# Attention and a gated feed-forward on one core: batch 3 by casting loads, batch 4's loads held until tile 2 runs, the tails of batches 0 and 1 moved ahead of batch 2's rounds

## The chip, the core and the metric

The kernel runs on one core of one Trainium2 chip. A core has five engines, each with an instruction stream of its own: TensorE (PE in the profile) multiplies matrices, VectorE (DVE), ScalarE (ACT) and GpSimd (POOL) work on elements, and SyncE (SP) here does nothing but issue DMA transfers. An engine runs its stream in order; if an instruction waits, everything behind it on the same engine waits too. Sixteen DMA engines move data between device memory and the core's on-chip memory (SBUF); the accumulators of TensorE lie in PSUM. The metric is device time in microseconds (us), lower is better. A time given for the kernel is the median of several executions.

## The reference

Eight batches, eight heads, 576 positions, head width 64. The inputs and the output are float32. Attention is causal by blocks of 64 positions, and its result is the input of a gated feed-forward:

```python
scores = (1 / sqrt(64)) * q @ k.transpose(0, 1, 3, 2)       # (8, 8, 576, 576)
scores = where(block_i >= block_j, scores, -1e9)            # blocks of 64 positions
attn   = exp(scores - max); attn = attn / (sum(attn) + 1e-9)
x      = (attn @ v), heads side by side                     # (8 * 576, 512)
gate   = maximum(x @ w_gate, 0)                             # w_gate: 512 x 1536
val    = x @ w_val                                          # w_val:  512 x 1536
out    = (gate * val) @ w_out                               # w_out: 1536 x 512
```

## The kernel before

**Units of work.** The first 512 positions of a batch are its main part, the last 64 its tail. Attention on the main part goes by head pairs: a *round* r = 4 * batch + pair covers two heads of one batch, 32 rounds in all. A round has scores (`visit`, L364: four chunks of keys by two heads, into PSUM tiles called `sc`, `one` and `ffnp`), exponentials on ScalarE (L387 for 512 columns of both heads, L393 for the rest), zeroing of the masked corners (L686, VectorE), products with v (`head_av`, L500, or `both_av`, L514; matmuls L491), a division by the row sums on VectorE (L456, L457) into a tile `xnat`, and a transpose of `xnat` into a quarter of `xT`, the feed-forward's input: on TensorE (`to_xT_pe`, L529) for batches 0 and 1, by a DMA transpose that SP issues (`to_xT_dma`, L540, recorded as L543) from batch 2 on. The tail of a batch is one visit for all heads (`tail_visit` L399, `tail_av` L464, matmuls L412 and L471), whose result goes by a DMA transpose (L485) into `xTt`.

**The feed-forward** runs in nine tiles (`ffn_gen`, L562): tile j below 8 is the main part of batch j, tile 8 all tails together. A tile has 96 matmuls of 512 columns for gate and val (L568; f runs over 12 slices of the 1536, c over the four quarters of `xT`) and 48 for the output (L625). ScalarE makes the relu (L578), VectorE the product gate * val, called `hT` (L583), and the copies of the output (L645, L656, L659), which ScalarE's queue stores (L554). In tiles 0 and 1 the first two slices are opened over quarters 0 and 1, then 2, then 3 of `xT`; from tile 2 on every slice needs all four quarters at once, so the fourth matmul of tile 2 needs the quarter of batch 2's last round.

**Order.** All engines run in the written order (`manual_schedule`, L691). The generator is a clock: one step is one feed-forward matmul, 144 steps a tile. `run(base, events)` (L780) sorts a list of (place, function) pairs and calls each function when the clock reaches base + place. A round is spread over such places by `round_at(p, r, av, to_xT, after)` (L785): scores and first exponentials at p, the others shortly after, products with v at `av`, the transpose at `to_xT`. `tail_at(p, b, av)` (L806) does it for a tail. Rounds 4 to 7 (batch 1) lie in the second half of tile 0, rounds 8 to 11 (batch 2) in tile 1, rounds 12 to 15 (batch 3) in tile 2, and so on: attention of batch j + 1 is laid between the matmuls of tile j.

**Loads.** There are two ways to bring a batch in.

- *Staged* (class `Early`, L107): SP issues plain float32 loads into a ring of ten `stage` tiles (L105), and POOL, ScalarE or VectorE cast them to bf16. `load_qk` (L127) takes q and k for n heads, `load_v` (L136) and `load_v_chunks` (L144) v, `load_tails` (L154) the last 64 rows. Batches 0 and 1 are then transposed on TensorE (`pe_mains` L232, `pe_tails` L251); batches 2 and 3 by DMA transposes on SP into tiles called `perm` (`transpose`, L205, recorded as L209; `transpose_tails`, L215) and, since q and k were loaded four positions to a row, put in order by copies on VectorE and POOL (`unpermute`, L221, recorded as L223).
- *Casting* (`load_qkv`, L264): POOL issues DMA transfers that read float32 and write bf16 (L276), five for each of q, k and v. SP then issues four DMA transposes (`dma_transposes`, L283): the main parts of q and k (L286), and their tails (L290). Batches 4 to 7 come this way; the loads of batch b + 1 are recorded in tile b - 1 at places 4 (q and k) and 46 (v), the transposes at 66. POOL has by then nothing else to do, so it runs ahead of the clock until something makes it wait.

SBUF buffers: `q_bf`/`k_bf` (L99) and their tails `q_bt`/`k_bt` (L102) have two buffers each, and `qTm`, `kTm`, `qTt`, `kTt` and `v_bf` two by batch parity, so that batch 3 takes what batch 1 used. `psum_ffn` has three banks, shared by gate, val, output, products with v and one part of each round's scores.

**Weights.** Gate and val weights come first, in halves; then batch 1's first four heads of q and k, `w_out` in three parts of two loads (`load_w_out`, L318; cast by `cast_w`, L321, the last quarter of the last part by VectorE at place 112.05), batch 1's v and its second four heads. In the kernel before, SP's order there is: two parts of `w_out`, v of heads 0 to 3, the third part, q and k of heads 4 to 7, v of heads 4 to 7, batch 0's tails, batch 2's q and k.

Of the kernel before, what the change touches and what calls it, by code (L numbers as in the profile page):

```python
# [12 lines left out]
AX = mybir.AluOpType  # L13
# [4 lines left out]
def kernel(  # L18
# [10 lines left out]
    nc = tc.nc  # L29
# [234 lines left out]
    def load_qkv(b, which):  # L264
        for t in which:
            src = (q, k, v)[t]
            for c in range(NCH):
                n = 128 if c < 4 else 64
                if t == 2:
                    dst = v_bf[b % 2][:n, c, :, 0:64]  # L270
                else:
                    if (b, 0) not in bfs:
                        bfs[b, 0], bfs[b, 1] = new_bf(), new_bt()
                    dst = bfs[b, 0][t][:, 512 * c : 512 * c + 512] if c < 4 else bfs[b, 1][t]
                    dst = dst.rearrange("p (h d) -> p h d", h=8)
                nc.gpsimd.dma_start(  # L276
                    dst,
                    src[b, :, 128 * c : 128 * c + n, :].rearrange("h p d -> p h d"),
                )

# [37 lines left out]
    def load_w_out(i):  # L318
        return load_w(wo[i], moe_w_out, 512 * i)
# [242 lines left out]
    def ffn_gen():  # L562
        for j in range(B + 1):
# [17 lines left out]
            def hidden(gate_sb, val):  # L581
                h = sb.tile([128, 512], BF, name="hT", bufs=13)
                nc.vector.tensor_tensor(out=h, in0=gate_sb, in1=val, op=AX.mult)  # L583
                hT.append(h)
# [106 lines left out]
    with tc.manual_schedule(engines={E.PE, E.DVE, E.Activation, E.Pool, E.SP}):  # L691
# [60 lines left out]
        w_out = [load_w_out(i) for i in range(2)]  # L752
        e1.load_v(0, 4)
        w_out.append(load_w_out(2))
        e1.load_qk(4, 4)
        e1.load_v(4, 4)
        e0.load_tails((0, 1))
        e0.load_tails((2,))
# [7 lines left out]
        e1.cast_v(0, 4, pool)  # L766
# [3 lines left out]
        e1.cast_qk(4, 4, (pool, None))  # L770
        e1.cast_v(4, 4, pool)
        e0.cast_tails((pool, pool))
        e0.cast_v_tail(pool)
# [57 lines left out]
        def tails_2():  # L831
            e1.cast_tails((pool, pool))
            e1.cast_v_tail(pool)
            e2.cast_tails((pool, pool))
            e2.transpose_tails()
            e2.cast_v_tail(pool)
# [4 lines left out]

        def load_3():
            e3 = early[3] = Early(3)
            e3.load_qk(0, 4)
            e3.load_tails((0, 1))
            e3.load_qk(4, 4)
            e3.load_tails((2,))
            e3.load_v_chunks(0)
            e3.load_v_chunks(1)

        def mains_3(h0):
            early[3].cast_qk(h0, 4, (pool, pool))
            if h0 == 4:
                early[3].cast_tails((pool, pool))

        def v_3():
            e3 = early[3]
            for g in range(2):
                e3.cast_v_chunks(g, pool)
            e3.cast_v_tail(pool)  # L860

        def un(b, hp, engs=(dve, dve)):
            return lambda: early[b].unpermute(hp, engs)

        def mains_2(h0):
            e2.load_v_chunks(h0 // 4)
            e2.cast_qk(h0, 4, (pool, pool))
            e2.transpose(h0 // 4)

        def load_tails():  # L870
            e1.load_tails((0, 1))
            e1.load_tails((2,))
            e2.load_tails((0, 1))
            e2.load_tails((2,))

        events = round_at(96, 4, (112, 112.1), (116, pe_xT), (6, 11))
        events += round_at(104, 5, (127, 127.1), (131, pe_xT), (6, 15))
        events += round_at(128.5, 6, (139, 140), (146, pe_xT), (4, 9))
# [6 lines left out]
            (120.2, lambda: e1.cast_qk(4, 4, (None, act))),  # L885
            (123, lambda: e1.pe_mains(2, (dve, act))),
            (125, lambda: e1.pe_mains(3, (dve, act))),
            (128, lambda: mains_2(0)),
            (142, lambda: e0.pe_tails((dve, act))),
            (143, lambda: mains_2(4)),  # L890
# [3 lines left out]
        events = tail_at(24, 0, (40, 44)) + tail_at(116, 1, (132, 136))  # L894
        for r, p in ((8, 41), (9, 58), (10, 75), (11, 92)):
            events += round_at(p, r, (p + 21, p + 25), (p + 25, to_xT_dma))
        events += [
            (88, lambda: e1.pe_tails((dve, act))),
            (20, lambda: store.pop()()),
            (25, un(2, 0, (dve, pool))),  # L900
            (28, un(2, 1, (dve, pool))),
            (46, v_2),
            (47, load_3),
            (52, un(2, 2, (dve, pool))),
            (56, un(2, 3, (dve, pool))),
            (60, tails_2),
            (66, lambda: mains_3(0)),
            (81, lambda: early[3].transpose(0)),
            (82, lambda: mains_3(4)),
            (101, lambda: early[3].transpose(1)),  # L910
            (118, lambda: early[3].transpose_tails()),
            (121, un(3, 0, (dve, pool))),
            (125, un(3, 1, (dve, pool))),
            (137, v_3),
        ]
        run(144, events)
        for b in range(3, B):
# [6 lines left out]
            if b == 3:  # L924
                events.append((2, un(3, 2, (dve, pool))))
                events.append((40, un(3, 3, (dve, pool))))
            if b + 1 < B:
                for at, which in ((4, (0, 1)), (46, (2,))):
                    events.append((at, lambda b=b, w=which: load_qkv(b + 1, w)))
                events.append((66, lambda b=b: dma_transposes(b + 1)))  # L930
# [31 lines left out]
```

The softmax here doesn't subtract the row's maximum and nothing guards it: scores larger than these inputs give would overflow.

## Time and profile before

| | |
|---|---|
| median of 9 runs | 374.96 us (371.48 to 376.3) |
| the profiled execution | 373.58 us, span 371.6 us, mean granted TensorE clock 0.998 |
| PE busy | 356.0 us, 96% of the span, 2963 matmuls |
| DVE, ACT, POOL busy | 174.9 us (47%), 169.8 us (46%), 112.7 us (30%) |
| device memory | 37.75 MB read, 9.44 MB written, 127 GB/s over the span |

The page shows one execution in several views: busy time by engine; the span in 40 slices; the DMA queues; the chain of work that ended last; the costliest groups of instructions with the idle time of the engine in front of them and what ended it; the DMA issues with their time to landing. Asked further, the trace gives the waits (who waited for whom), a timeline of one engine in a window, busy time by window, and single DMA issues. "SPq" and "POOLq" are issuing queues. A matmul of 512 columns is shown at about 379 ns, but successive ones overlap: 96 of them in a row take 20.72 us in the chain, 0.2158 us each. That 0.2158 us is one step of the clock of the order above where nothing else lies between.

With that step, tile 0 starts at 17.78 us in the timeline of TensorE, tile 1 at 61.24, tile 2 at 104.57 and tile 3 at 148.83. From there each tile takes about 38.8 us (in the chain, the first matmul of tile 4 is at 189.56 and that of tile 5 at 228.33).

### The profile page before, as it was taken

What the parts mean: (1) busy time and instruction counts of PE and PEld (TensorE: products, weight loads), DVE (VectorE), ACT (ScalarE), POOL (GpSimd) and SP (SyncE); (2) the same over time, 40 slices, a digit from 0 to 9 for tenths busy, and PEclk for the clock granted to TensorE, in tenths of its full rate; (3) what the DMA queues carried; (4) which work ended last, traced back from release to release, by engine and by line L of the source; (5) the groups of instructions that cost most, each with busy time, mean ns of one, the idle gap of its engine ahead of it and who ended that gap; (6) DMA issues with size and microseconds to landing.
All of it is one profiled execution on the core that took longest, in us unless ns stands there. A gap on an engine that the chain in (4) does not pass through costs nothing.

```text
span 371.6 us, 7467 instructions
## 1 busy us (share of the span) xinstructions
PE 356.0 (96%) x2963; PEld 176.5 (47%) x2963; DVE 174.9 (47%) x399; ACT 169.8 (46%) x278; POOL 112.7 (30%) x142
## 2 busy tenths in 40 slices
PE   6799989999969999899999999999999999999996
PEld 2444445544534545344554455444544454444443
DVE  4744465775534554354345533554354543423432
ACT  5733746667235652456445544553465323302310
POOL 5776645285079920930066004000000000000000
PEclk9999999999999999999999999999999999999999
DMA  8999999999889999997499747956200120020014
GB/s 253 279 347 357 319 258 311 211 203 248 136 155 127 119 145 163 162 126 142 114 96 138 125 115 86 57 77 137 79 17 14 56 88 7 0 86 28 0 36 108
DMA packets 145187, 51.35 MB, mean 138 GB/s; under 512 B 124544, under 2 KB 139136, under 8 KB 145152
## 3 DMA queue, kind: packets, MB, share of 16 engines
q1 hardware_dynamic: 83616, 34.62, 43.6%
q0 software_dynamic: 56256, 7.08, 38.5%
q10 hardware_dynamic: 5280, 9.18, 7.7%
q8 instruction: 23, 0.38, 0.5%
q14 instruction: 12, 0.10, 0.1%
HBM read 37.75 MB, written 9.44 MB: 127 GB/s over the span
## 4 chain that ended last, share of the span: by engine, by line
PE 80%; DMA 15%; SPq 1%; ACT 1%; issue 0%; POOL 0%; DVE 0%; ACTq 0%; POOLq 0%
PE ffnp L568 45%; PE ffnp L625 22%; DMA stage<-in_moe_w_gate_dram 5%; PE ffnp L491 4%; DMA xT<-xnat 4%; DMA stage<-in_k_dram 3%; PE sc L378 3%; DMA stage<-in_moe_w_out_dram 3%; PE ffnp L471 2%; PE one L378 1%; SPq L139 1%; DMA stage<-in_v_dram 1%; PE sc L412 1%; PE one L412 0%; ACT gate_sb L578 0%
## 5 line engine op out<-in xcount | busy, mean ns | idle before, releaser
L583 DVE TENSOR_TENSOR hT<-gate_sb,ffnp 128x512 bf16<-128x512 bf16 x106 | 72.8, 687 | 95.7 <-PE ffnp L568 83.5
L578 ACT ACTIVATE gate_sb<-ffnp 128x512 bf16<-128x512 f32 x108 | 64.7, 601 | 105.4 <-PE ffnp L568 101.8
L568 PE MATMUL ffnp<-xT,wg 128*128 128x512 bf16 x384 | 103.7, 379 | 6.1 <-DMA xT<-xnat 4.7
L625 PE MATMUL ffnp<-wo,hT 128*128 128x512 bf16 (+1 forms) x444 | 102.0, 373 | 0.2 <-DVE ob L645 0.2
L568 PE MATMUL ffnp<-xT,wv 128*128 128x512 bf16 x376 | 100.5, 379 | 0.0
L568 PEld LDWEIGHTS <-wg 128*128 128x128 bf16 x432 | 40.2, 98 | 48.9 <-issue 5.3
L568 PEld LDWEIGHTS <-wv 128*128 128x128 bf16 x432 | 40.0, 98 | 49.2 <-issue 6.1
L625 PEld LDWEIGHTS <-hT 128*128 128x128 bf16 x444 | 40.5, 98 | 41.5 <-issue 0.8
L387 ACT ACTIVATE attnT<-sc 128x1024 bf16<-128x1024 f32 x56 | 57.0, 1039 | 0.2 <-issue 0.2
L659 DVE COPY ob<-ffnp 128x512 f32<-128x512 f32 (+1 forms) x35 | 23.7, 677 | 39.1 <-PE ffnp L625 39.1
L276 POOL DMA_DIRECT2D v_bf<-in_v_dram x20 | 17.2, 882 | 67.5 <-PE ffnp L471 67.5
L491 PEld LDWEIGHTS <-attnT 128*128 128x128 bf16 x640 | 26.2, 98 | 14.0 <-DVE xnat L457 3.5
L456 DVE RECIPROCAL recip<-ffnp 128x4 f32<-128x4 f32 (+1 forms) x73 | 13.1, 179 | 33.3 <-PE ffnp L491 21.5
L491 PE MATMUL ffnp<-v_bf,attnT 128*128 128x65 bf16 x570 | 26.4, 194 | 0.0
L393 ACT ACTIVATE attnT<-one 128x256 bf16<-128x256 f32 x28 | 10.7, 383 | 33.7 <-PE ffnp L378 28.8
L457 DVE TENSOR_TENSOR xnat<-ffnp,recip 128x256 bf16<-128x256 f32 x57 | 24.2, 424 | 2.5 <-DMA xT<-xnat 0.5
L433 ACT ACTIVATE attnTt<-one 64x256 bf16<-64x256 f32 x8 | 3.0, 377 | 33.5 <-PE ffnp L412 26.9
L378 PE MATMUL sc<-qTm,kTm 64*128 64x512 bf16 (+1 forms) x168 | 17.4, 305 | 0.0
L378 PEld LDWEIGHTS <-kTm 64*128 64x128 bf16 x224 | 9.6, 94 | 15.6 <-issue 11.7
L424 ACT ACTIVATE attnTt<-sc 128x1024 bf16<-128x1024 f32 x16 | 15.6, 1013 | 0.0
L223 POOL COPY kTm<-perm 128x512 bf16<-128x512 bf16 x8 | 9.2, 1175 | 19.0 <-DMA perm<-k_bf 13.6
L276 POOL DMA_DIRECT2D k_bf<-in_k_dram x16 | 14.3, 935 | 0.6 <-DMA v_bf<-in_v_dram 0.3
(87 smaller groups left out, 263.9 us busy)
## 6 DMA issues: line engine op xcount, KB each, us to landing
out_dram<-ob ACTq DMA_DIRECT2D x32, 256.0 KB, 2.7
stage<-in_moe_w_gate_dram SPq DMA_DIRECT2D x6, 512.0 KB, 8.9
stage<-in_moe_w_val_dram SPq DMA_DIRECT2D x6, 512.0 KB, 8.7
stage<-in_q_dram SPq DMA_DIRECT2D x6, 512.0 KB, 6.5
stage<-in_k_dram SPq DMA_DIRECT2D x6, 512.0 KB, 6.7
stage<-in_moe_w_out_dram SPq DMA_DIRECT2D x6, 512.0 KB, 8.6
stage<-in_v_dram SPq DMA_DIRECT2D x20, 128.0 KB, 5.7
stage<-in_v_dram SPq DMA_DIRECT2D x8, 256.0 KB, 6.5
```

The costliest lines, as they stand in the source:

```text
L276: nc.gpsimd.dma_start(dst, src[b, :, 128 * c : 128 * c + n, :].rearrange("h p d -> p h d"),)
L378: nc.tensor.matmul(where[c].rearrange("p (c n) -> p c n", n=128), kTm[b % 2][head_of(hh), c, hp, :], qTm[b % 2][head_of(hh), c:4, hp, :], ...
L387: return lambda: nc.scalar.activation(at[:, :, lo : lo + 512], sc, AF.Exp, scale=scale)
L424: return lambda: nc.scalar.activation(at[:, :, 2 * i : 2 * i + 2, 0:256], main[i].rearrange("p g (h n) -> p g h n", h=2), AF.Exp, scale=scale,
L456: nc.vector.reciprocal(recip, av[:, :, 64])
L457: nc.vector.tensor_tensor(out=out, in0=av[:, :, 0:64], in1=recip.to_broadcast([rows, n, 64]), op=AX.mult,)
L491: nc.tensor.matmul(av[:, p, :], at[:, col : col + 128], v_bf[b % 2][:, c, h, :], start=(p == 0), stop=(c == p), skip_group_check=True,)
L568: nc.tensor.matmul(to, (wg, wv)[t][f // 4][:, c, 128 * (f % 4) : 128 * (f % 4) + 128], x[:, c], start=(c == 0), stop=(c == 3),)
L578: nc.scalar.activation(gate_sb, gate, AF.Relu)
L583: nc.vector.tensor_tensor(out=h, in0=gate_sb, in1=val, op=AX.mult)
L625: nc.tensor.matmul(op, hT[f][:, 128 * s : 128 * (s + 1)], wo[f // 4][:, f % 4, n0:n1], start=(f == lo), stop=(f == hi - 1),)
L659: nc.vector.tensor_copy(ob, op)
```

## The change

The changed kernel loads batch 3 as batches 4 to 7 are loaded, by casting DMA on POOL and four DMA transposes on SP, recorded in tile 1 (q and k at place 59, v at 92, the transposes at 119). `load_3`, `mains_3`, `v_3` and batch 3's un-permuting copies go. The casting loads of batch 4's q and k are recorded at place 9 of tile 2 instead of 4, and the first of them waits for the VectorE product (`hT`) recorded last before it. The tails of batches 0 and 1 are both loaded, cast and transposed before tile 1, and their attention lies at places 24 and 40 of tile 1 (before: 24 and 116); batch 2's rounds begin at 54, 67, 80 and 94 (before: 41, 58, 75, 92). All of `w_out` is loaded and cast ahead of batch 1's v. Batch 1's second four heads of q and k are loaded and cast two at a time; the products with v of round 4 move from place 112 to 120, round 6 from 128.5 to 126, the transposes of head pair 3 from 125 to 129. The un-permuting copies of batch 2 move from places 25, 28, 52, 56 to 43, 46, 50, 56, its tails from 60 to 90.

```diff
--- before.py
+++ after.py
@@ -261,7 +261,9 @@
             for t in range(2):
                 evac[t]((qTt, kTt)[t][self.b % 2][:, 0:4, :], tp[:, t])
 
-    def load_qkv(b, which):
+    products = []
+
+    def load_qkv(b, which, behind=None):
         for t in which:
             src = (q, k, v)[t]
             for c in range(NCH):
@@ -273,10 +275,12 @@
                         bfs[b, 0], bfs[b, 1] = new_bf(), new_bt()
                     dst = bfs[b, 0][t][:, 512 * c : 512 * c + 512] if c < 4 else bfs[b, 1][t]
                     dst = dst.rearrange("p (h d) -> p h d", h=8)
-                nc.gpsimd.dma_start(
+                ins = nc.gpsimd.dma_start(
                     dst,
                     src[b, :, 128 * c : 128 * c + n, :].rearrange("h p d -> p h d"),
                 )
+                after(ins, behind)
+                behind = None
 
     bfs = {}
 
@@ -580,7 +584,9 @@
 
             def hidden(gate_sb, val):
                 h = sb.tile([128, 512], BF, name="hT", bufs=13)
-                nc.vector.tensor_tensor(out=h, in0=gate_sb, in1=val, op=AX.mult)
+                products.append(
+                    nc.vector.tensor_tensor(out=h, in0=gate_sb, in1=val, op=AX.mult)
+                )
                 hT.append(h)
 
             first = 0
@@ -749,13 +755,14 @@
         e1, e2 = Early(1), Early(2)
         e1.load_qk(0, 4)
         ffn(23)
-        w_out = [load_w_out(i) for i in range(2)]
+        w_out = [load_w_out(i) for i in range(3)]
         e1.load_v(0, 4)
-        w_out.append(load_w_out(2))
-        e1.load_qk(4, 4)
+        for h0 in (4, 6):
+            e1.load_qk(h0, 2)
         e1.load_v(4, 4)
-        e0.load_tails((0, 1))
-        e0.load_tails((2,))
+        for e in (e0, e1):
+            e.load_tails((0, 1))
+            e.load_tails((2,))
         e2.load_qk(0, 4)
         e2.load_qk(4, 4)
         for g in range(2):
@@ -763,14 +770,16 @@
         e1.cast_qk(0, 4, (pool, None))
         cast_w(w_out[0], pool)
         cast_w(w_out[1], pool)
-        e1.cast_v(0, 4, pool)
         cast_w(w_out[2][:1], pool)
         last_w = [[a[:, c : c + 1] for a in w_out[2][1]] for c in range(2)]
         cast_w(last_w[:1], pool)
-        e1.cast_qk(4, 4, (pool, None))
+        e1.cast_v(0, 4, pool)
+        for h0 in (4, 6):
+            e1.cast_qk(h0, 2, (pool, None))
         e1.cast_v(4, 4, pool)
-        e0.cast_tails((pool, pool))
-        e0.cast_v_tail(pool)
+        for e in (e0, e1):
+            e.cast_tails((pool, pool))
+            e.cast_v_tail(pool)
         place = [32]
 
         def upto(p):
@@ -829,8 +838,6 @@
         early = {2: e2}
 
         def tails_2():
-            e1.cast_tails((pool, pool))
-            e1.cast_v_tail(pool)
             e2.cast_tails((pool, pool))
             e2.transpose_tails()
             e2.cast_v_tail(pool)
@@ -838,26 +845,6 @@
         def v_2():
             e2.cast_v_chunks(0, pool)
             e2.cast_v_chunks(1, pool)
-
-        def load_3():
-            e3 = early[3] = Early(3)
-            e3.load_qk(0, 4)
-            e3.load_tails((0, 1))
-            e3.load_qk(4, 4)
-            e3.load_tails((2,))
-            e3.load_v_chunks(0)
-            e3.load_v_chunks(1)
-
-        def mains_3(h0):
-            early[3].cast_qk(h0, 4, (pool, pool))
-            if h0 == 4:
-                early[3].cast_tails((pool, pool))
-
-        def v_3():
-            e3 = early[3]
-            for g in range(2):
-                e3.cast_v_chunks(g, pool)
-            e3.cast_v_tail(pool)
 
         def un(b, hp, engs=(dve, dve)):
             return lambda: early[b].unpermute(hp, engs)
@@ -868,50 +855,43 @@
             e2.transpose(h0 // 4)
 
         def load_tails():
-            e1.load_tails((0, 1))
-            e1.load_tails((2,))
             e2.load_tails((0, 1))
             e2.load_tails((2,))
 
-        events = round_at(96, 4, (112, 112.1), (116, pe_xT), (6, 11))
+        events = round_at(96, 4, (120, 120.1), (125, pe_xT), (6, 11))
         events += round_at(104, 5, (127, 127.1), (131, pe_xT), (6, 15))
-        events += round_at(128.5, 6, (139, 140), (146, pe_xT), (4, 9))
+        events += round_at(126, 6, (138.2, 139), (146, pe_xT), (4, 9))
         events += round_at(138, 7, (148, None), (153, pe_xT), (3, 8))
         events += [
             (80, lambda: e1.cast_qk(0, 4, (None, dve))),
             (93, lambda: e1.pe_mains(0, (dve, act))),
             (95, lambda: e1.pe_mains(1, (dve, act))),
             (112.05, lambda: cast_w(last_w[1:], dve)),
-            (120.2, lambda: e1.cast_qk(4, 4, (None, act))),
+            (119, lambda: e1.cast_qk(4, 2, (None, act))),
+            (120.2, lambda: e1.cast_qk(6, 2, (None, act))),
             (123, lambda: e1.pe_mains(2, (dve, act))),
-            (125, lambda: e1.pe_mains(3, (dve, act))),
+            (129, lambda: e1.pe_mains(3, (dve, act))),
             (128, lambda: mains_2(0)),
             (142, lambda: e0.pe_tails((dve, act))),
+            (142, lambda: e1.pe_tails((dve, act))),
             (143, lambda: mains_2(4)),
             (143, load_tails),
         ]
         run(0, events)
-        events = tail_at(24, 0, (40, 44)) + tail_at(116, 1, (132, 136))
-        for r, p in ((8, 41), (9, 58), (10, 75), (11, 92)):
-            events += round_at(p, r, (p + 21, p + 25), (p + 25, to_xT_dma))
+        events = tail_at(24, 0, (37, 39)) + tail_at(40, 1, (55, 58))
+        for r, p in ((8, 54), (9, 67), (10, 80), (11, 94)):
+            events += round_at(p, r, (p + 21, p + 24), (p + 24, to_xT_dma))
         events += [
-            (88, lambda: e1.pe_tails((dve, act))),
             (20, lambda: store.pop()()),
-            (25, un(2, 0, (dve, pool))),
-            (28, un(2, 1, (dve, pool))),
-            (46, v_2),
-            (47, load_3),
-            (52, un(2, 2, (dve, pool))),
+            (43, un(2, 0, (dve, pool))),
+            (46, un(2, 1, (dve, pool))),
+            (46.5, v_2),
+            (50, un(2, 2, (dve, pool))),
             (56, un(2, 3, (dve, pool))),
-            (60, tails_2),
-            (66, lambda: mains_3(0)),
-            (81, lambda: early[3].transpose(0)),
-            (82, lambda: mains_3(4)),
-            (101, lambda: early[3].transpose(1)),
-            (118, lambda: early[3].transpose_tails()),
-            (121, un(3, 0, (dve, pool))),
-            (125, un(3, 1, (dve, pool))),
-            (137, v_3),
+            (59, lambda: load_qkv(3, (0, 1))),
+            (90, tails_2),
+            (92, lambda: load_qkv(3, (2,))),
+            (119, lambda: dma_transposes(3)),
         ]
         run(144, events)
         for b in range(3, B):
@@ -921,12 +901,16 @@
             for i, p in enumerate((27, 50, 73, 96) if b == 3 else (2, 32, 62, 92)):
                 r = 4 * b + i
                 events += round_at(p, r, (p + 20, p + 24), (p + 24, to_xT_dma))
-            if b == 3:
-                events.append((2, un(3, 2, (dve, pool))))
-                events.append((40, un(3, 3, (dve, pool))))
             if b + 1 < B:
-                for at, which in ((4, (0, 1)), (46, (2,))):
-                    events.append((at, lambda b=b, w=which: load_qkv(b + 1, w)))
+                for at, which in ((9, (0, 1)), (46, (2,))):
+                    events.append(
+                        (
+                            at,
+                            lambda b=b, w=which: load_qkv(
+                                b + 1, w, products[-1] if b == 3 and w == (0, 1) else None
+                            ),
+                        )
+                    )
                 events.append((66, lambda b=b: dma_transposes(b + 1)))
             run(144 * (b - 1), events)
         ffn(10**6)
```

## The prediction

> **What bounds the kernel now.** I read the page's busy shares first, then TensorE's waits, its timeline where they lie, and SP's timeline over the longest.
>
> ```profile
> PE 356.0 (96%) x2963; PEld 176.5 (47%) x2963; DVE 174.9 (47%) x399; ACT 169.8 (46%) x278; POOL 112.7 (30%) x142
> ```
>
> TensorE is the bound. The change keeps every matmul, so it can only give or take idle time in front of them; TensorE's waits name what there is.
>
> ```profile
> PE ffnp L568 <- DMA xT<-xnat: 4.7, 4, 3.2
> ...
> PE ffnp L568 <- POOL wg L323: 1.0, 1, 1.0
> PE ffnp L238 <- ACT k_bf L168: 0.8, 1, 0.8
> ```
>
> TensorE's timeline (start, us, instruction, idle before):
>
> ```profile
> 47.57 1.25 PE L625 MATMUL ffnp<-wo,hT 128*128 128x512 bf16 x4 [0.17 <-DVE ob L645]
> 49.00 0.40 PE L537 MATMUL ffnp<-ident,xnat 128*128 128x128 bf16 x4 [0.18 <-DVE xnat L457]
> ...
> 51.96 0.40 PE L238 MATMUL ffnp<-ident,k_bf 128*128 128x128 bf16 x4 [0.83 <-ACT k_bf L168]
> ...
> 109.25 0.38 PE L568 MATMUL ffnp<-xT,wg 128*128 128x512 bf16 x1 [3.18 <-DMA xT<-xnat]
> ...
> 149.63 0.38 PE L568 MATMUL ffnp<-xT,wg 128*128 128x512 bf16 x1 [0.42 <-DMA xT<-xnat]
> ...
> 151.55 0.38 PE L568 MATMUL ffnp<-xT,wg 128*128 128x512 bf16 x1 [0.89 <-DMA xT<-xnat]
> 152.17 0.38 PE L568 MATMUL ffnp<-xT,wg 128*128 128x512 bf16 x1 [0.24 <-DMA xT<-xnat]
> ```
>
> The big one is the fourth matmul of tile 2, which waits for round 11's quarter of xT. Its xnat was ready at 98.37 (VectorE's timeline: L457 at 97.95 for 0.42). SP's timeline shows why it came late:
>
> ```profile
> 83.35 6.50 SPq L149 DMA_DIRECT2D stage<-in_v_dram  x4
> 89.95 1.76 SPq L217 DMA_TRANSPOSE qTt<-q_bt  x1
> 91.81 2.02 SPq L217 DMA_TRANSPOSE kTt<-k_bt  x1
> 93.93 1.22 SPq L543 DMA_TRANSPOSE xT<-xnat  x1
> 95.24 1.26 SPq L209 DMA_TRANSPOSE perm<-q_bf  x1
> 96.59 1.29 SPq L209 DMA_TRANSPOSE perm<-k_bf  x1
> 97.97 3.57 SPq L543 DMA_TRANSPOSE xT<-xnat  x2
> 101.63 1.26 SPq L209 DMA_TRANSPOSE perm<-q_bf  x1
> 102.99 1.53 SPq L209 DMA_TRANSPOSE perm<-k_bf  x1
> 104.61 2.24 SPq L543 DMA_TRANSPOSE xT<-xnat  x1
> ```
>
> SP is issuing without a gap, mostly for batch 3, and round 11's transpose starts 6.24 us after its data. It lands 4.6 us later. The transfer is ordinary; the queue is the loss. At tile 3 (1.55 us) the same engine is held by batch 4's transposes:
>
> ```profile
> 125.37 4.74 SPq L286 DMA_TRANSPOSE qTm<-q_bf  x1
> ...
> 131.63 6.51 SPq L286 DMA_TRANSPOSE kTm<-k_bf  x1
> ...
> 168.27 1.86 SPq L286 DMA_TRANSPOSE qTm<-q_bf  x1
> ...
> 172.13 2.02 SPq L286 DMA_TRANSPOSE kTm<-k_bf  x1
> ```
>
> The first pair lies beside batch 5's casting loads (POOL issues them from 124.19 to 134.5) and lands after 12.1 and 12.6 us; the second pair, batch 5's, lies beside none and lands after 4.4 and 5.9.
>
> **Batch 3 by casting loads: SP.** Off SP before round 11 go ten loads of batch 3 (from 77.71 to 89.85: 0.58, 0.50, 0.63, 0.63, 0.63, 1.10, 1.11 and 6.50, that is 11.7 us) and four perm transposes (5.3 us); two tail transposes (2.4 us) were behind round 11 and stay there, joined by the two new large ones. Ahead of it stay batch 2's two tail transposes and three xT transposes. So round 11 is issued when ready. Its second products with v now lie at place 118, 26 steps or 5.6 us before tile 2 (no tail of batch 1 in between any more); less 0.6 us for products and division, it is issued 5.0 us before tile 2. xT transposes issued from 93.9 to 104.6 landed after 2.4 to 4.7 us: arrival 2.6 to 0.3 us before tile 2, and it is needed 0.65 us after its start. I take the whole 3.2 us away. The other end is nothing gained, by the 8.8 us that round 15's took at 143.31 in crowded queues: 5.0 - 8.8 is 3.8 us late, less 0.65: 3.2 again.
>
> **POOL's side.** POOL loses 4 + 2 + 3 casts and four kTm copies of batch 3 and gains 15 issues, 8.7 us for q and k and 4.6 for v (rows of batch 4: 3.65, 0.73, 3.55, 0.77, 4.63). They follow batch 2's last kTm copy, which ended at 79.78 and may come 2 us sooner, since tail 0 is read earlier and its v buffer frees. Three tail casts of batch 2 (1.8 us) are queued between, and behind them batch 2's tail transposes on SP, ahead of round 9's xT: done by some 90 and 94, when round 9 is ready at 88 to 91. Batch 3's v is issued by 93 to 95 and, at the 4.7 to 5.7 us of batch 4's v, landed at 98 to 101, about when round 11 is issued at 99. The hold is what keeps batch 4 out: without it POOL would go on at 95. It releases after the first product of tile 2, 2.9 us into it; queued behind are batch 4's q, k, v and batch 5's q and k. Before, batch 4's started 0.9 us after TensorE went on; now about 1.3 us later by the same clock, but without the 1.15 us kTm copy at 118.58. Batch 5's thus overlap batch 4's transposes as before, and I keep the 1.55 us at tile 3 and add 0.3 (ends: -1.5 and +1.0, what the 1.3 us could do undiluted).
>
> **Batch 3's transposes** follow round 11 on SP, from about 100: at the quick rows 1.9 + 1.7 us, then kTm from 104 landing after 4.3 to 6.3, by 110.5. Round 12's scores come 8.0 us after tile 2's start (115.76 - 104.57, less the 3.18), near 112. Nothing lost; rival 2 has the other end.
>
> **wo ahead of v, loads by head pairs (tile 0).** Two w_out loads (2.3 us on SP) pass four v loads (6.2 us): bytes in front of q and k are unchanged, v is landed where w_out was, by 46.9, cast by 48, and round 4 now wants it near 48.9. Four loads for two add 0.9 us on SP and 0.2 us on POOL and ACT each. The k that TensorE waited for landed in one 512 KB piece at 50.45, q at 48.87; of the halves the first pair is there by 48.9, cast by ACT (0.62 us) at 49.5, wanted at 50.4: the 0.83 goes, and the 0.18. Late next: the second pair, cast at 51.1, holds ACT's copy of the first kTm to 51.7, round 6's scores wait about 0.2; and the eleventh slice of w_out (VectorE casts it at 47.9, after two output copies), where round 4's products no longer cover: 0.6 idle against 0.4 before. Tails of batch 1 now follow batch 0's on SP, in front of batch 2's loads: 3 issues (2 us), 3 casts (1.9 us). Batch 2's un-permuting has moved later by more than that (place 25 to 43, 18 steps, 3.9 us). But batch 1's k tail is issued near 54, takes the 4.8 us of batch 0's, is cast at 59.3, and TensorE asks at about 59.3: 0 to 0.6 idle, I take 0.2. Sum for tile 0: -0.83 - 0.18 + 0.2 + 0.2 + 0.2, or -0.4 (ends -1.0 and +0.5).
>
> **Tile 1, rounds closer.** From place 39 to 64 VectorE has four un-permuting copies, three hT products (0.69 each), two tail divisions (0.6 each) and a corner (0.3): at the copies' mean of 1.03, 7.7 us, while TensorE has 25 steps, one round's scores (0.65) and two tail products (0.6 each), 7.2 us, and needs hT done before banks return. The copies span 0.55 to 1.40, so -1.4 to +2.0 against that; buffers of three banks absorb some. ScalarE needs 2.6 us for a round's exponentials and 1.0 for relus per 13 steps of 4.2 us: it fits. Before, tile 1 lost 0.23 in front of 85.97. I take +0.3 (ends -0.3 and +1.5).
>
> A rule weighs on this: the Trainium skill, "SBUF — State Buffer", section "Who interferes with whom", says that a VectorE copy in a two-port mode and a GpSimd instruction shut each other out for the whole instruction. The trace agrees: two such copies took 2.73 us beside POOL's at 68.93 and 1.10 us alone at 98.99. By the rule each of the four could wait for a POOL instruction of 1.04 us, and this term would be about 1.3 instead of 0.3.
>
> **Sum.** -3.2 - 0.4 + 0.3 + 0.3 = -3.0 us against the profiled execution (373.58, span 371.6 and 2.0 around it): 370.6. The median shown is 1.38 higher, so 372.0. What 0.5% means, about what can be told apart: 373.1 to 376.8.
>
> **Rivals.**
>
> 1. *The transfer is late again, not the issue.* For it: 8.8 to 10.6 us for the xT transposes near 140, beside casting loads, which now also run in tile 1. Against: these were issued while casting loads were still being issued; batch 3's v will have been issued some 5 us before. Gain at tile 2 zero, the rest stays: 375.2.
> 2. *Batch 3's transposes are late (slower).* At batch 4's rows they run 4.74 + 1.24 us, kTm is issued at 106.4 and lands 12.6 later, 119.0; round 12 wants it at 112: 7.1 us idle, 379.1. For it: batch 4's held loads are issued from about 106.5, beside kTm. Against: qTm is through by then and eight loads are still to come, where batch 4's met ten from the start. It decides from a landing at 115: 3 us late, the whole gain.
> 3. *Tile 1 becomes dense.* VectorE's backlog passes to TensorE by the upper ends, +1.5 in tile 1 and +1.0 at tile 3 instead of 0.3 each: 373.9.
>
> That the hold does nothing is excluded by POOL's order: it would be free some 10 us earlier.
>
> **Chances.** Forecast 0.62, rival 1 0.12, rival 2 0.12, rival 3 0.14. A part of rival 3 stays faster (0.04): faster 0.66. Same: rival 1 and the rest of 3, 0.22. Slower: 0.12. The likeliest one's own range is 370.5 to 373.4 (half of the summed ends of tiles 0, 1 and 3, -3.0 and +2.8 around the values taken, since they hardly fall together). Rival 2 would lie wholly above; 8 in 10 takes rivals 1 and 3 in: 370.0 to 376.2.
>
> **What would show it.** Right: no idle above 0.5 us on xT in front of the fourth matmul of tile 2; SP with gaps before round 11's transpose, issued within 1 us of its division; the 0.83 on k_bf gone; about 1.5 to 2 us on xT still at tile 3; POOL idle until the first product of tile 2. Wrong: TensorE waiting at round 12's scores for qTm or kTm; waits on hT or xtail between places 40 and 66; round 11's transpose over 6 us in flight.

## The result, and the profile after

The changed kernel takes 370.33 us (median of 17 runs, 368.47 to 372.92), the kernel before 374.84 (52 runs, 371.48 to 378.62). The ratio is 0.9898 [0.9878, 0.9918]: 3.8 us less. It is formed over the fast executions alone and is not the quotient of the two medians, which differ by 4.5 us. The forecast was 372.0, with 370.0 to 376.2 around it; the result lies near the low end, 0.2 us below the 370.5 to 373.4 that the prediction gave its likeliest case. The profiled execution takes 370.03 us with a span of 368.2, against 373.58 and 371.6.

The page of the kernel after, busy shares and then the chain by engine:

```profile
PE 358.3 (97%) x2963; PEld 177.4 (48%) x2963; DVE 170.6 (46%) x395; ACT 169.8 (46%) x279; POOL 113.7 (31%) x145
...
PE 92%; DVE 2%; DMA 2%; ACT 1%; issue 0%; POOL 0%; ACTq 0%; POOLq 0%
```

TensorE still bounds the kernel, with the same 2963 matmuls and less idle time (in the same row of before, the chain has 80% on TensorE and 15% on DMA). TensorE's waits, after (us in total, times, longest):

```profile
PE ffnp L572 <- DMA xT<-xnat: 1.2, 2, 1.0
...
PE ffnp L631 <- DVE wo L327: 0.5, 1, 0.5
PE ffnp L631 <- DVE ob L662: 0.4, 1, 0.4
```

The waits on xT have gone from 4.7 us to 1.2; 0.5 on a cast of `w_out` is new. The same, in TensorE's timeline of the kernel after (L572 and L631 are L568 and L625 of before):

```profile
48.42 1.24 PE L631 MATMUL ffnp<-wo,hT 128*128 128x512 bf16 x5 [0.47 <-DVE wo L327]
50.69 0.81 PE L631 MATMUL ffnp<-wo,hT 128*128 128x512 bf16 x3 [0.41 <-DVE ob L662]
51.88 0.38 PE L238 MATMUL ffnp<-ident,k_bf 128*128 128x128 bf16 x4 [0.17 <-DVE xnat L461]
...
104.55 0.81 PE L572 MATMUL ffnp<-xT,wg 128*128 128x512 bf16 x3
...
105.99 0.39 PE L572 MATMUL ffnp<-xT,wg 128*128 128x512 bf16 x1
...
147.57 0.38 PE L572 MATMUL ffnp<-xT,wg 128*128 128x512 bf16 x1 [0.24 <-DMA xT<-xnat]
...
148.91 0.38 PE L572 MATMUL ffnp<-xT,wg 128*128 128x512 bf16 x1 [0.96 <-DMA xT<-xnat]
```

The fourth matmul of tile 2 (105.99) has no idle in front; between it and the third lies only a tail's scores. SP's timeline, after:

```profile
99.81 1.20 SPq L547 DMA_TRANSPOSE xT<-xnat  x1
...
101.20 1.63 SPq L290 DMA_TRANSPOSE qTm<-q_bf  x1
102.94 2.19 SPq L294 DMA_TRANSPOSE qTt<-q_bt  x1
105.31 2.15 SPq L290 DMA_TRANSPOSE kTm<-k_bf  x1
```

Round 11's division ends at 99.78, and SP issues the transpose 0.03 us later (before: 6.24). It lands after 3.6 us, at 103.4. Batch 3's kTm is issued at 105.31 and lands after 4.4, at 109.7; round 12's scores ask at 112.51. POOL, after, issues batch 3's last load by 94.07 and batch 4's first one only at 108.91:

```profile
89.83 4.24 POOL L278 DMA_DIRECT2D v_bf<-in_v_dram  x5
108.91 3.52 POOL L278 DMA_DIRECT2D q_bf<-in_q_dram  x4 [14.85 <-issue]
```

Where the 3.40 us of span went, from the first matmul of each tile in TensorE's timelines:

| | before | after | difference |
|---|---|---|---|
| start of tile 1 | 61.24 | 61.64 | +0.40 |
| tile 1 | 43.33 | 42.91 | -0.42 |
| tile 2 | 44.26 | 41.28 | -2.98 |
| tile 3, up to the end of its waits on xT | 3.34 | 3.08 | -0.26 |
| from there to the end | 219.43 | 219.29 | -0.14 |

The first row holds 0.52 us of a later start: batch 1's second pair of q transposes at 41.12, before at 40.60. Most of it, 0.38, is there at the start of tile 0 (18.16, before 17.78), ahead of everything that was changed; over the ten traces of this case that start lies between 16.84 and 18.16. Tensor work of 0.34 us (`pe_tails` of batch 1, from 88.17 in the chain before) moved from tile 1 into tile 0, so tile 1 itself changed by -0.08.

### The profile page after: what moved, and what is told of

It reads as the page before. It is cut to its first block, busy times and chain, and to the rows that moved or that the text cites. A ratio compares the mean times of both kernels' runs of the same rounds, so it can differ in the third digit from the quotient of the medians.

```text
span 368.2 us, 7461 instructions
## 1 busy us (share of the span) xinstructions
PE 358.3 (97%) x2963; PEld 177.4 (48%) x2963; DVE 170.6 (46%) x395; ACT 169.8 (46%) x279; POOL 113.7 (31%) x145
## 4 chain that ended last, share of the span: by engine, by line
PE 92%; DVE 2%; DMA 2%; ACT 1%; issue 0%; POOL 0%; ACTq 0%; POOLq 0%
PE ffnp L572 51%; PE ffnp L631 24%; PE ffnp L495 5%; PE sc L382 3%; PE ffnp L475 2%; DMA xT<-xnat 2%; PE one L382 1%; PE ffnp L238 1%; PE sc L416 1%; PE sc L339 1%; PE ffnp L685 1%; ACT attnT L355 1%; DVE xnat L461 1%; PE sc L572 0%; PE one L416 0%
## 5 line engine op out<-in xcount | busy, mean ns | idle before, releaser
L572 PE MATMUL ffnp<-xT,wg 128*128 128x512 bf16 x384 | 103.7, 379 | 1.4 <-DMA xT<-xnat 1.2
L631 PE MATMUL ffnp<-wo,hT 128*128 128x512 bf16 (+1 forms) x444 | 101.5, 373 | 0.9 <-DVE wo L327 0.5
L572 PE MATMUL ffnp<-xT,wv 128*128 128x512 bf16 x376 | 101.2, 379 | 0.0
L572 PEld LDWEIGHTS <-wg 128*128 128x128 bf16 x432 | 40.2, 98 | 46.7 <-issue 4.2
L572 PEld LDWEIGHTS <-wv 128*128 128x128 bf16 x432 | 39.9, 98 | 46.5 <-issue 3.6
L631 PEld LDWEIGHTS <-hT 128*128 128x128 bf16 x444 | 40.9, 98 | 42.8 <-issue 1.9
L278 POOL DMA_DIRECT2D v_bf<-in_v_dram x25 | 21.1, 882 | 62.5 <-PE ffnp L475 62.5
L278 POOL DMA_DIRECT2D q_bf<-in_q_dram x20 | 18.3, 953 | 15.2 <-issue 14.8
L278 POOL DMA_DIRECT2D k_bf<-in_k_dram x20 | 17.8, 924 | 1.8 <-DMA v_bf<-in_v_dram 1.3
```

What stands on the lines that cost most here:

```text
L278: ins = nc.gpsimd.dma_start(dst, src[b, :, 128 * c : 128 * c + n, :].rearrange("h p d -> p h d"),)
L572: nc.tensor.matmul(to, (wg, wv)[t][f // 4][:, c, 128 * (f % 4) : 128 * (f % 4) + 128], x[:, c], start=(c == 0), stop=(c == 3),)
L631: nc.tensor.matmul(op, hT[f][:, 128 * s : 128 * (s + 1)], wo[f // 4][:, f % 4, n0:n1], start=(f == lo), stop=(f == hi - 1),)
```

## The experiments

The theory: the gain is SP's queue in front of round 11's transpose, taken away by loading batch 3 on POOL. The rivals: any later perm transpose would do it; the hold, or tile 1's new order, does no work; tile 0's part carries the gain. All ratios are to the kernel before, measured beside it.

### Batch 3 staged again, all else as in the kernel after

```diff
-(59, lambda: load_qkv(3, (0, 1))),
-(90, tails_2),
-(92, lambda: load_qkv(3, (2,))),
-(119, lambda: dma_transposes(3)),
+(47, load_3),
+(60, tails_2),
+(66, lambda: mains_3(0)),
+(81, lambda: early[3].transpose(0)),
...
+(101, lambda: early[3].transpose(1)),
+(118.5, lambda: early[3].transpose_tails()),
+(121, un(3, 0, (dve, pool))),
...
```

The casts, the other un-permuting copies and `v_3` are at the places of before too.

> The changed kernel with one part undone: batch 3 is again loaded by SP and cast and put in order by POOL and VectorE, at the places of before; everything else stays. If SP's queue is what made round 11's transpose late, SP is full again from about 78 to 109 us, that transpose is issued 4 us or more after its division, and TensorE waits about 2 to 3 us on xT in tile 2: ratio to before about 0.997 (0.993 to 1.000), against 0.990 for the whole change. If instead the new places of the rounds and tails in tile 1 brought the gain, it stays near 0.990 and the wait in tile 2 stays under 0.5 us.

1.0076 [1.0045, 1.0106], median 376.92. SP's timeline, batch 3 staged again:

```profile
84.35 7.97 SPq L149 DMA_DIRECT2D stage<-in_v_dram  x4
...
97.40 1.22 SPq L547 DMA_TRANSPOSE xT<-xnat  x1
...
101.71 1.22 SPq L547 DMA_TRANSPOSE xT<-xnat  x1
...
106.45 2.61 SPq L547 DMA_TRANSPOSE xT<-xnat  x2
```

and TensorE's timeline of the same kernel:

```profile
100.57 5.35 PE L631 MATMUL ffnp<-wo,hT 128*128 128x512 bf16 x23 [2.33 <-DVE xnat L461]
...
109.11 0.38 PE L572 MATMUL ffnp<-xT,wg 128*128 128x512 bf16 x1 [2.77 <-DMA xT<-xnat]
```

The queue is full again and the wait is back: round 11's division ends at 101.05, and its transpose is through SP only at 109.06. It is worse than before: batch 2's transposes are so late that VectorE finds no free `xnat` (three buffers) and TensorE waits 2.33 us for a division. So casting batch 3 is the part that pays, and the new rounds' order without it loses. The size was missed: a gain of 0.3% was expected, 0.8% was lost.

### The kernel before, with only the second pair's perm transposes moved behind round 11's

```diff
-(101, lambda: early[3].transpose(1)),
+(117.5, lambda: early[3].transpose(1)),
...
-events.append((2, un(3, 2, (dve, pool))))
+events.append((20, un(3, 2, (dve, pool))))
```

> The kernel before with two DMA transposes moved on SP: the second pair of batch 3's perm transposes from place 101 to behind round 11's xT transpose, and the un-permuting copies that use them from place 2 to 20 of tile 2. If SP's queue is the loss, round 11's transpose is issued about 2.9 us sooner (near 101.7), the 3.18 us in tile 2 shrink to 0.3 to 1.0, and the ratio to before is 0.993 to 0.995. If the transfer itself is slow (crowded DMA engines), it lands as late as before and the ratio is 1.000.

0.9959 [0.9928, 0.9989], median 372.80. SP's timeline of this kernel:

```profile
101.06 5.08 SPq L543 DMA_TRANSPOSE xT<-xnat  x3
106.24 1.26 SPq L209 DMA_TRANSPOSE perm<-q_bf  x1
```

and TensorE's timeline at the start of tile 2:

```profile
107.57 0.81 PE L568 MATMUL ffnp<-xT,wg 128*128 128x512 bf16 x3
...
109.00 0.39 PE L568 MATMUL ffnp<-xT,wg 128*128 128x512 bf16 x1
```

The last of three is through at 106.1, and tile 2 (from 107.57 in this execution) runs without a wait in 41.20 us, as in the kernel after (41.28). Two DMA issues moved by 16.5 steps, with the copies that use them, remove the whole wait. So the place of SP's issues is the cause, and casting loads are one way to free it. The time gained is smaller, 1.5 us by the ratio, a little less than expected; the profiled execution lost 1.27 and 1.54 us in tile 0, on casts of q and k, at places that the edit does not touch. That made TensorE 3.0 us later at tile 2, but round 11's division came 3.0 us later too (101.36, before 98.37), so the late start is not what removed the wait.

### The kernel after, without the hold

```diff
-b + 1, w, products[-1] if b == 3 and w == (0, 1) else None
+b + 1, w, None
```

> The changed kernel without the hold: batch 4's casting loads of q and k wait for no product and POOL goes on with them at about 94 us. If the hold carries part of the gain, ten casting loads are in flight from 94 to 108, beside round 11's transpose and batch 3's four: round 11's lands after 6 to 10 us instead of some 3 to 5, TensorE waits 1 to 3 us in tile 2, perhaps also at round 12's scores; ratio to before 0.993 to 0.999. If free SP is all that matters, it stays at 0.990 and xT shows no wait in tile 2.

1.0131 [1.0091, 1.0171], median 378.88. POOL, not held, goes on with batch 4's q and k:

```profile
94.34 3.62 POOL L278 DMA_DIRECT2D q_bf<-in_q_dram  x4
```

TensorE's timeline:

```profile
108.77 0.59 PE L572 MATMUL ffnp<-xT,wg 128*128 128x512 bf16 x1 [3.19 <-DMA xT<-xnat]
...
121.15 0.28 PE L382 MATMUL one<-qTm,kTm 64*128 64x256 bf16 x1 [2.89 <-DMA kTm<-k_bf]
```

SP's timeline of the same kernel:

```profile
99.34 1.22 SPq L547 DMA_TRANSPOSE xT<-xnat  x1
100.75 7.46 SPq L290 DMA_TRANSPOSE qTm<-q_bf  x1
```

SP issues round 11's transpose in time, but it is 9.4 us in flight beside the casting loads (with the hold: 3.6), so the same idle as before returns with another cause. qTm takes 13.5 us to land (4.8), kTm 11.4 (4.4). These are the prediction's rivals 1 and 2, both at once. The hold is a condition of the gain; I had expected this kernel to stay faster than before.

### The kernel after, with the hold for every batch

```diff
-b + 1, w, products[-1] if b == 3 and w == (0, 1) else None
+b + 1, w, products[-1] if w == (0, 1) else None
```

> The changed kernel with the hold on the q and k loads of every later batch too, not of batch 4 alone. The wait on xT at the start of tile 3 (1.2 us after the change, 1.55 before) is put down to SP issuing batch 4's transposes slowly beside batch 5's casting loads. If that is so, with batch 5's loads held until tile 3 those transposes take 1.6 to 2.2 us of SP each for the large ones instead of 5.0 and 6.6, the three xT transposes behind them land in time, and the 1.2 us go: ratio to before 0.986 to 0.988. If the wait has another cause, 0.990; if the held loads come too late for the transposes, slower than 0.990, with TensorE waiting on qTm or kTm at a first round of a batch.

0.9832 [0.9798, 0.9866], median 368.04. Batch 5's q and k, at 121.37 in the kernel after, are now issued at 149.32, behind batch 4's transposes. SP's timeline:

```profile
121.96 4.54 SPq L290 DMA_TRANSPOSE qTm<-q_bf  x1
...
127.97 2.69 SPq L290 DMA_TRANSPOSE kTm<-k_bf  x1
```

They land after 8.3 and 4.3 us (12.8 and 13.5 in the kernel after), and TensorE waits for no xT anywhere. From tile 3's start to the end is 1.66 us shorter, 1.20 of it the two waits. The remaining stall had the cause named for it, casting loads beside DMA transposes, and the gain is larger than the 0.986 to 0.988 expected.

### The kernel before, with the hold for every casting batch

```diff
-for at, which in ((4, (0, 1)), (46, (2,))):
-    events.append((at, lambda b=b, w=which: load_qkv(b + 1, w)))
+for at, which in ((9, (0, 1)), (46, (2,))):
...
+b + 1, w, products[-1] if w == (0, 1) else None
```

`products` and `behind` are as in the kernel after.

> The kernel before with the hold alone, on the q and k loads of every casting batch, at place 9; batch 3 staged as before. Batch 5's loads then wait until tile 3 runs, batch 4's transposes are quick and the 1.55 us on xT at tile 3 go, while the 3.2 us at tile 2, which come from SP's staged loads, stay: ratio 0.995 to 0.997. If both waits had one cause, casting loads beside transposes, the 3.2 would shrink as well: 0.990 or less.

0.9998 [0.9964, 1.0032], median 374.05: the gain of 0.3 to 0.5% that was expected does not show in the time. The trace divides it. Tile 3 has no wait, as with the hold in the kernel after, and from its start to the end it is 1.93 us shorter than before; tile 2's wait stays, since its cause is SP's queue:

```profile
109.46 0.59 PE L572 MATMUL ffnp<-xT,wg 128*128 128x512 bf16 x1 [3.64 <-DMA xT<-xnat]
```

That idle was followed by half the granted clock (last section), which made tile 2 of this execution 46.74 us instead of 44.26. Whether the other executions lost the gain in the same way is not known.

### The kernel after, with tile 1 in its old order

```diff
-events = tail_at(24, 0, (37, 39)) + tail_at(40, 1, (55, 58))
-for r, p in ((8, 54), (9, 67), (10, 80), (11, 94)):
+events = tail_at(24, 0, (40, 44)) + tail_at(116, 1, (132, 136))
+for r, p in ((8, 41), (9, 58), (10, 75), (11, 92)):
...
-(92, lambda: load_qkv(3, (2,))),
+(137, lambda: load_qkv(3, (2,))),
```

Batch 2's un-permuting copies go back to 25, 28, 52 and 56.

> The changed kernel with the order in tile 1 of before: tail of batch 1 at place 116, rounds 8 to 11 at 41, 58, 75 and 92, the un-permuting copies early; batch 3's v is loaded behind that tail, at place 137, because it takes the tail's buffer. If SP's relief is all, round 11's transpose is still issued when ready and the ratio stays at 0.990. If the order is there to get batch 3's casting loads out of the way, its v is now in flight at 103 to 112 us, beside batch 3's transposes, with batch 4's following: the large transposes take 4 us of SP or more and land after 10, round 12's scores wait 1 to 4 us, ratio 0.993 to 1.001.

1.0032 [1.0003, 1.0061], median 376.14. Round 11's transfer is in time, and the loss moves to eight microseconds into tile 2. POOL's timeline of this kernel:

```profile
102.61 4.19 POOL L278 DMA_DIRECT2D v_bf<-in_v_dram  x5 [12.73 <-PE ffnp L475]
```

and TensorE's:

```profile
115.04 0.39 PE L382 MATMUL one<-qTm,kTm 64*128 64x256 bf16 x1 [3.02 <-DMA kTm<-k_bf]
```

Batch 3's v takes batch 1's buffer. With batch 1's tail at 116, its products with v end late, POOL waits 12.73 us for them, and the loads run beside kTm, which is issued at 104.20 and lands after 10.8 us (after: 4.4). So what the early tails give here is the free v buffer, which puts the loads ahead of the transposes; no other gain from the new order shows.

### The kernel before, with tile 0's part alone

```diff
-w_out = [load_w_out(i) for i in range(2)]
+w_out = [load_w_out(i) for i in range(3)]
 e1.load_v(0, 4)
-w_out.append(load_w_out(2))
-e1.load_qk(4, 4)
+for h0 in (4, 6):
+    e1.load_qk(h0, 2)
...
-events = round_at(96, 4, (112, 112.1), (116, pe_xT), (6, 11))
+events = round_at(96, 4, (120, 120.1), (125, pe_xT), (6, 11))
```

The casts follow the loads' order, round 6 starts at 126, and head pair 3's transposes lie at 129, as in the kernel after. The tails stay where they were.

> The kernel before with the part in tile 0 alone: all of w_out ahead of batch 1's v, q and k of its second four heads two at a time, round 4's products, round 6 and the transposes of head pair 3 at their new places; tails and tile 1 as before. The prediction gave this part 0.4 us, mostly the 0.83 on the cast of k; the profile of the changed kernel shows that wait gone and 0.9 us of new ones on the last quarter of w_out. Ratio to before 0.997 to 1.000, waits in tile 2 and tile 3 unchanged at some 3 and 1.5 us. If the part were worth more than it looks, 0.995 or less.

1.0003 [0.9976, 1.003], median 374.97. TensorE's timeline:

```profile
48.11 1.24 PE L625 MATMUL ffnp<-wo,hT 128*128 128x512 bf16 x5 [1.02 <-DVE wo L323]
50.37 0.81 PE L625 MATMUL ffnp<-wo,hT 128*128 128x512 bf16 x3 [0.41 <-DVE ob L656]
51.57 0.38 PE L238 MATMUL ffnp<-ident,k_bf 128*128 128x128 bf16 x4 [0.16 <-ACT k_bf L168]
```

The wait on k_bf is down from 0.83 to 0.16, and 1.02 on the `w_out` cast has come. From the second pair's q transposes to tile 1 it is 20.65 us, before 20.64: nothing gained. VectorE's timeline says why, of the kernel before:

```profile
47.98 0.42 DVE L323 CAST wo<-stage 128x512 bf16<-128x512 f32 x1
```

and of this one:

```profile
47.08 0.97 DVE L323 CAST wo<-stage 128x512 bf16<-128x512 f32 x1
```

and POOL's timeline of this one:

```profile
46.73 1.05 POOL L181 CAST v_bf<-stage 128x1024 bf16<-128x1024 f32 x1 [1.22 <-DMA stage<-in_v_dram]
```

The cast took 0.42 us in the kernel before, from 47.98, while POOL did nothing between 47.48 and 48.87. Here it is recorded from 47.08 for 0.97, while POOL casts v from 46.73 to 47.78; before, that cast of v ran at 44.02, and the change has put it here. In the profiled execution of the kernel after, POOL's v cast ran 46.47 to 47.52, and VectorE's, recorded from 47.95, took 0.42.

### The hold for every batch, and the last quarter of w_out cast by POOL

```diff
-cast_w(last_w[:1], pool)
+cast_w(last_w, pool)
...
-(112.05, lambda: cast_w(last_w[1:], dve)),
...
-b + 1, w, products[-1] if b == 3 and w == (0, 1) else None
+b + 1, w, products[-1] if w == (0, 1) else None
```

> The changed kernel with the hold on all casting batches, and the last quarter of w_out cast by POOL right behind its other quarter instead of by VectorE behind two output copies. POOL was idle there for 1.3 us, so TensorE's wait of 0.5 to 1.0 us on that cast goes and nothing is added; the 0.4 us on the next output copy may stay. Ratio 0.981 to 0.983 where the hold on all batches alone measured 0.983; if POOL's later casts of v and q slip by the 0.6 us into the path, no gain, 0.983 to 0.985.

0.9799 [0.976, 0.9839], median 366.97 (366.76 to 367.69), span 364.9. TensorE's timeline:

```profile
48.60 0.81 PE L631 MATMUL ffnp<-wo,hT 128*128 128x512 bf16 x3 [0.27 <-DVE ob L662]
49.79 0.38 PE L238 MATMUL ffnp<-ident,k_bf 128*128 128x128 bf16 x4 [0.16 <-DVE xnat L461]
51.42 0.28 PE L382 MATMUL one<-qTm,kTm 64*128 64x256 bf16 x1 [0.38 <-ACT kTm L244]
```

The wait on the cast is gone; 0.38 on a copy of kTm follows (the 0.2 that the prediction had there). This is the best version of all, 3.4 us below the kernel after and a little better than expected. Its interval overlaps that of the hold for every batch alone, so of the 1.1 us between these two medians the trace shows the cause and the times do not show the size.

## Why the prediction was right, and where it was off

- **Tile 2, -3.2: right.** The row says -2.98, the wait is gone for the reason given, and both undoing the load path and moving two issues confirm SP's queue. "Issued when ready" held to 0.03 us, and the forecast landing (2.6 to 0.3 us before tile 2) came out as 1.1 before it.
- **The hold: right as an argument from POOL's order, not priced.** The sum took "keeps batch 4 out" as given and gave no value to what it prevents. Without it the kernel is 8.5 us slower by the medians. The rows for that price were at hand: 8.8 to 10.6 us in flight beside casting loads, in the rival that got 0.12.
- **Batch 3's transposes, 0: right.** kTm landed at 109.7, forecast by 110.5, and 2.8 us before it was asked for. Rival 2 needed the loads beside the transposes; two experiments show the mechanism and a wait of about 3 us.
- **Tile 1, +0.3: too dear.** It came to -0.08. No wait on hT or xtail appears between places 40 and 66, and the 0.23 of before is gone. The larger value, 1.3, which the lock of the two-port copies would have given there, did not come about in this tile: one un-permuting copy took 1.22 us beside a copy on POOL (at 77.18; another, with none beside it, 0.59), but TensorE did not wait. How 1.3 follows from four waits of 1.04 us, the prediction does not say.
- **Tile 3, +0.3: wrong sign, small.** The waits were 1.20 us instead of 1.55, also below the 1.5 to 2 that the prediction named as a sign of being right. Batch 4's loads began 4.36 us into tile 2, where I had put them at 2.9, and still did no harm to it. The end of -1.5 is what the hold for all batches then delivered.
- **Tile 0, -0.4: the step that failed is the term for `w_out`, "0.6 idle against 0.4 before".** The wait on the cast alone is 0.5 to 1.1 us: 0.47 in the kernel after, 0.81 without the hold, 0.99 with the hold for all, 1.02 with tile 0 alone, 1.13 with the old tile 1. Less the 0.34 of moved tails, the stretch to tile 1 changed by -0.46, -0.13, +0.05, +0.01 (there no tails moved) and +0.20 in the same order. With batch 3 staged again the wait was 0.47 and the change -0.42. So my -0.4 was met by the two executions with a cast of 0.42 us; over the six the mean is -0.13. With that quarter cast by POOL the change was -0.66. I priced the arrival of the slice and not the engine beside it. The rule cited for tile 1, the Trainium skill's "SBUF — State Buffer", section "Who interferes with whom", speaks of casts in a two-port mode too: the engine that comes second is shut out for the whole instruction. The rows agree: casts of 0.76 to 1.07 us where POOL's v cast had begun first, each ending 0.27 or 0.28 us after POOL's, and 0.42 where VectorE began first or POOL's was over. (In the kernel after, POOL's next cast, of q, lasted to 48.08, 0.13 us into VectorE's; the 0.42 does not show that it cost anything.)
- **From the profiled execution to the median: the largest miss.** Of the 1.63 us between 371.96 (the forecast before rounding) and 370.33, 0.55 is the sum (370.58 against 370.03). The other 1.08 is the difference of 1.38 between the profiled execution of before and its median, which I carried over as if it belonged to every kernel; after, it is 0.30. The last section has the probable cause.
- **The sum: near the mark in part by luck.** In the span it was off by 0.40 us, because its misses cancel: tiles 1 and 3 came out 0.38 and 0.56 us better than taken and the rest of the kernel 0.14, while tile 2 gave 0.22 less and 0.52 of a later start was in no term. The prediction counts ten loads of batch 3 ahead of round 11; the rows hold eleven, whose 11.7 us it adds up rightly.

## What to carry to other kernels

When a consumer waits for a DMA, first compare the time from data to issue with the time from issue to landing: 6.24 and 4.6 us here said that the issuing queue was at fault, and that the remedy was to free it. Loads moved to another queue can still slow the transfers that the critical engine awaits (round 11's took 9.4 us beside them and 3.6 without), so loads that can run ahead need a hold until those are through; here taking the hold away cost 8.5 us by the medians, more than the 4.5 that the whole change gains. Where a cast or copy of VectorE feeds the critical engine, look at what GpSimd does in the same microsecond before taking its duration from a quiet place.

## What was not expected of the hardware

After some idles of TensorE the granted clock fell to one half for microseconds. The view by stretches, of the kernel before (from, to, length, then busy us of TensorE, its weight loads, VectorE, ScalarE and POOL, then the granted clock, the DMA share and GB/s), around its idle of 3.18 us:

```profile
108.00:110.00 2.00, 0.75 (x4) 0.38 (x4) 0.00 (x0) 0.34 (x1) 0.86 (x1) 1.00 0.65 96
110.00:112.00 2.00, 2.00 (x11) 0.88 (x9) 0.69 (x1) 1.77 (x3) 2.00 (x3) 1.00 0.21 34
112.00:114.00 2.00, 2.00 (x28) 1.24 (x27) 0.75 (x2) 0.60 (x1) 2.00 (x4) 1.00 1.58 101
```

and of the kernel with tile 0's part alone, around the same idle, there 3.78 us:

```profile
108.00:110.00 2.00, 0.32 (x1) 0.10 (x1) 0.00 (x0) 0.00 (x0) 0.44 (x1) 0.50 0.95 133
110.00:112.00 2.00, 1.78 (x5) 0.76 (x5) 0.00 (x0) 1.51 (x2) 2.00 (x3) 0.50 0.21 37
112.00:114.00 2.00, 2.00 (x6) 0.70 (x5) 0.69 (x1) 0.28 (x1) 2.00 (x3) 0.50 1.16 74
114.00:116.00 2.00, 2.00 (x9) 0.79 (x8) 0.69 (x1) 0.32 (x1) 2.00 (x4) 0.81 2.04 130
```

The clock stays at 1.00 in the first and stands at 0.50 from 108 to 114 in the second. Tile 2 took 47.36 us there: 41.28 as in the kernel after, 3.78 idle, and 2.30 more. In the other experiments idles of 3.64, 3.19, 3.02 and 2.89 us, and one of 2.77 with 0.40 behind it, were each followed by stretches at 0.50, as were two of 1.27 and 1.54 in short succession; the 3.18 of before and one of 2.33 were not. The Trainium skill, "TensorE: Matmul & The Clock Gate", section "Part 1: The HAM clock gate (the "warmup" mystery)", has half the clock follow an idle window of about 3.4 us that runs freely, so that it depends on where an idle falls; the rows agree in the two values of the clock and in the uncertain onset, and show it for idles somewhat shorter than that too.

So the wait at tile 2 costs either its own 3 to 4 us or some 2 more. That would explain three things: why the median of before lies above its profiled execution, which kept the full clock; why its times spread over 7.1 us (52 runs), those of the kernel after over 4.5 (17), and those of the best version, which has no idle of TensorE over 0.4 us from tile 0's output on, over 0.9 (only 6); and why the measured gain of 3.8 us is above the sum's 3.0.

Of each kernel one execution has a trace, but the mean granted clock is on record for others too. Traces with one stretch at 0.50 have a mean of 0.995, with two 0.991 or 0.986, with three 0.982. Of 50 executions of the kernel before, measured beside the experiments, 25 have 0.991 or less, with a median of 375.3 us, 20 have 0.995 (373.8) and 5 have 0.998 or more (372.9). Of the 17 of the kernel after, only 2 have 0.991 or less, and 7 have 0.998 or more. So the kernel before does lose clock more often, and its executions that lose more are slower. That they lose it at tile 2 is argued and not shown: in five of the ten traces a stretch at 0.50 lies between 8 and 14 us as well, ahead of everything that was changed.
